# Two transformer layers on one core: packing the attention output for three of its four output projections

## The chip, the core and the metric

The kernel runs on one core of a Trainium2 chip. The core has a matrix engine (TensorE, "PE" in the profile; its weight loads are shown apart as "PEld"), three engines that work on vectors (VectorE or DVE, ScalarE or ACT, GpSimd or POOL) and a queue engine, SyncE or SP, which here issues almost all transfers. Each engine runs its own instructions in the order of the program and waits on semaphores for the others. TensorE writes its results to PSUM, which has eight banks of 128 partitions by 512 floats. The metric is the device time of one execution in microseconds, the median of the runs shown.

## The reference

The input x has 2048 rows of 448 floats. Twice, with the same weights, it goes through an attention layer and a gated feed-forward layer:

```
x = x + A(layernorm(x));  x = x + B(layernorm(x));  x = x + A(layernorm(x));  x = x + B(layernorm(x))

A(x): q = x @ wq            16 heads of 28
      k = x @ wk, v = x @ wv  one head of 28, shared by all query heads
      p = softmax(q k^T / sqrt(28));  o = p v
      return concat(o) @ wo   (448 -> 448)
B(x): (silu(x @ w_gate) * (x @ w_up)) @ w_down   (448 -> 1792 -> 448)
```

The change concerns the last line of A, `concat(o) @ wo`, and the norm behind it.

## The kernel before, in words

**Attention.** The 2048 rows are cut into four chunks of 512 rows (c = 0..3), and the 16 heads into four groups of four heads. A chunk and a head group make one of the 16 entries of `GR`; the loop in `scores` calls them i = 4c + g, and this text calls an entry a group. For each group the loop makes 16 steps (kt = 0..15), one for each block of 128 keys, so a layer has 256 steps, numbered n = 16 i + kt. A step makes the scores of four heads (`step`, L639: twelve matmuls, each in a strip of 32 rows of the array), and ScalarE takes their exponential: three heads at once from the PSUM tile `three` (L646, L652), the fourth from a bank of its own (L651 in even steps; in odd steps VectorE copies it to `raw`, L648, and ScalarE reads that, L649). Two steps make a pair d. `pv` (L680) multiplies the exponentials of the pair before by the values and VectorE adds the result to the group's accumulator `o` (L687 for the first pair, L690 after it). A column of ones beside the values makes the 29th row of each head the softmax's sum.

**The end of a group.** `post` (L701) sends the four rows of sums to `rs` over SP's queue. Three pairs later, at kt = 5 of the following group, `rest` runs: VectorE makes five short checks and a reciprocal of `rs` (L707 to L709), SP sends it out and brings it back spread over the partitions (`rd<-rs` L711, `o<-rd` L712), and GpSimd multiplies (L719) and splits the result into a rounded high part and a low part (`split`, L139 and L140). In before they go to `onh` and `onl`, in the row block of the group: head j of the group stands in partitions 32j to 32j+27, and the four partitions behind it are spare.

**Output projection.** When the last group of a chunk is through, the chunk is put on `todo`. `between(d)`, which is called at the end of each odd step, takes it off at kt = 10 and issues `outproj` for the four tiles of 128 rows: 4 head groups x 3 products (high x high, high x low, low x high) = 12 matmuls a tile over 128 partitions, whose spare rows meet zeros in `woh` and `wol`; 48 matmuls in all (L622), followed by four additions to the residual `xres` on VectorE (L626). They stand in the program between two pairs. This happens for the chunks 0, 1, 2, in groups 4, 8 and 12. The fourth chunk's projection comes after the loop and is not part of the change, apart from the name of its tile. The weights come in at kt = 8 of groups 2 and 3 (`load_wo`): GpSimd clears the buffer `wr`, SP loads it in four transfers, GpSimd splits it.

**The next norm.** The table `later` holds, by step number, the parts of the feed-forward's norm of a chunk: four `stat` steps on VectorE (L240, L241), `scale` on GpSimd (`rstd`, L246 and L247), four times `apply` (L255) and `turn` (a transpose, L260) on VectorE, then `send` and `load` over SP's queue and, for chunks 0 and 1, eight conversions on VectorE. In before they begin at the first step of the group behind the projection, 16 (4c + 5).

**What sets the order.** Each engine keeps the order in which the code issues. Transfers of SP's queue are issued in that order too; an SP instruction that waits holds back those behind it. The queries of a group come over the same queue: `stack(i + 2)` loads `qraw` at kt = 12 (L443), `parts(i + 1)` splits it on GpSimd at kt = 0, and `rows(i + 1)` adds four rows at kt = 3 (L454). In groups 11, 12 and 13 `weights` loads feed-forward weights at kt = 8 into the same `wr` and splits them in twelve GpSimd instructions.

Of the kernel before, what the change touches and what calls it, by code (L numbers as in the profile page):

```python
# [9 lines left out]
F32R = mybir.dt.float32r  # L10
AF = mybir.ActivationFunctionType
ALU = mybir.AluOpType
# [40 lines left out]
def forward(  # L53
# [315 lines left out]
    class Attention:  # L369
# [230 lines left out]
        def scores(self, ff):  # L600
            next(switch)
            with tc.tile_pool(name=f"at{self.layer}", bufs=1, reuse_waits="tile") as wp:
# [3 lines left out]
                todo, due = [], {}  # L606
                single = lambda d: banks[6 + d % 2]

                def load_wo(z):
                    r = wpool.tile([P, 4, 2, P], F32, name="wr").rearrange("p (z k) b n -> p z (k b n)", z=2)  # L610
                    nc.gpsimd.memset(r, 0.0)
                    for j in range(4):
                        nc.sync.dma_start(r[32 * j : 32 * j + DH, :, 0:D], wos[j][:, 2 * z : 2 * z + 2, :])
                    zs = slice(2 * z, 2 * z + 2)
                    split(woh[:, zs, :], wol[:, zs, :], r[:, :, 0:D])

                def outproj(c, t, po, gs=range(NG)):
                    oh, ol = on[c]
                    ts_ = slice(P * t, P * t + P)
                    for g in gs:  # L620
                        for z, (a, b) in enumerate(((oh, woh), (oh, wol), (ol, woh))):
                            nc.tensor.matmul(  # L622
                                po[:, 0:D], a[:, g, ts_], b[:, g, :], start=(g + z == 0), stop=(g == NG - 1 and z == 2)
                            )
# [69 lines left out]
                def post(i):  # L694

                    c, g = GR[i]
                    out2 = accs.pop(i)
                    oraw, rb = out2[:, 0, :], out2[:, 1, :]
                    rs = wp.tile([P, 16], F32, name="rs", bufs=2)
                    for j in range(4):  # L700
                        nc.sync.dma_start(rs[32 * j : 32 * j + 32, :], oraw[32 * j + DH : 32 * j + DH + 1, :])  # L701

                    def rest():
                        if fine is not None:
                            under = wp.tile([P, 16], F32, name="under", bufs=2)
# [5 lines left out]
                        nc.sync.dma_start(rd.rearrange("j (p n) -> (j p) n", n=16), rs)  # L711
                        nc.sync.dma_start(rb, rd[:, None, :].to_broadcast([4, 32, 512]))  # L712
                        if g == 0:
                            on[c] = (
                                wp.tile([P, NG, 512], F32R, name="onh"),
                                wp.tile([P, NG, 512], F32R, name="onl"),
                            )
                        oh, ol = on[c]
                        nc.gpsimd.tensor_tensor(rb, oraw, rb, ALU.mult)  # L719
# [21 lines left out]
                for n in range(last):  # L741
# [580 lines left out]
```

## Time and profile before

| | |
|---|---|
| median of three runs | 1959.17 us (1959.09 to 1959.79) |
| the profiled execution's own time | 1959.78 us |
| its span, first to last instruction | 1958.0 us |
| share of the span in which TensorE is busy | 99% |
| ScalarE | 68% |
| VectorE | 52% |
| GpSimd | 40% |

The shares are averages over stages of different kinds. In the first layer the 256 attention steps lie between 61 and 565 us of the span, in the second between 1031 and 1535 us; the rest is projections of queries and the feed-forward layers. "Busy" for TensorE counts overlapping matmuls whose ends are modelled, so 99% does not say that it never waits: it is read together with what the other engines wait for.

### The profile page before, as it was taken

The page shows a single profiled execution, that of the slowest core. Times are in us where ns is not written, and L with a number is a line of the kernel's source. Part 1 is how long each engine was busy: PE and PEld are TensorE (multiplying, and loading weights), DVE is VectorE, ACT ScalarE, POOL GpSimd, SP SyncE. Part 2 cuts the span into 40 slices and gives each one's busy share as a digit, 9 for nine tenths or more (in the row PEclk, how much of TensorE's full clock was granted, in tenths as well). Part 3 has the DMA queues.
Part 4 walks back from the last instruction along what each step waited for, and adds up shares of the span by engine and source line. Part 5 has one row for each costly group of instructions (what it writes and reads, how often), then busy time and mean ns, then how long its engine had stood idle before and what let it go on. Part 6 is the DMA issues. An engine that isn't in the chain of part 4 may idle for free. (4 is left out here: it accounts for less than half of the span.)

```text
span 1958.0 us, 45644 instructions
## 1 busy us (share of the span) xinstructions
PE 1946.5 (99%) x18307; PEld 1312.0 (67%) x18307; DVE 1016.5 (52%) x1711; ACT 1338.3 (68%) x2353; POOL 774.2 (40%) x997
## 2 busy tenths in 40 slices
PE   9999999999999999999999999999999999999998
PEld 8544545445458899999984444454454688999997
DVE  7444543544425567665654335445454346666653
ACT  4899797998963344444349998979979533444432
POOL 5212111132314868766441221111232167688640
PEclk9999999999999999999999999999999999999999
DMA  5110020121210110111131011102121101110002
GB/s 167 54 30 26 23 49 22 31 59 28 73 33 2 53 32 21 28 32 27 52 114 33 27 31 31 45 12 62 30 53 48 33 7 48 33 32 22 27 17 77
DMA packets 100017, 79.69 MB, mean 41 GB/s; under 512 B 26040, under 2 KB 83000, under 8 KB 99800
## 3 DMA queue, kind: packets, MB, share of 16 engines
q1 hardware_dynamic: 99224, 75.81, 14.2%
q8 instruction: 144, 2.36, 0.5%
q10 hardware_dynamic: 576, 0.92, 0.1%
q14 instruction: 73, 0.60, 0.1%
HBM read 57.15 MB, written 18.74 MB: 39 GB/s over the span
## 5 line engine op out<-in xcount | busy, mean ns | idle before, releaser
L680 PE MATMUL bank<-pt,vsb 128*32 128x512 f32 x4096 | 493.3, 598 | 0.3
L639 PE MATMUL bank<-qstack,keys 32*128 32x512 f32 x1536 | 484.5, 425 | 0.0
L639 PE MATMUL three<-qstack,keys 32*128 32x512 f32 x4608 | 460.2, 425 | 1.5 <-DVE vt L573 1.2
L639 PEld LDWEIGHTS three<-qstack,keys 32*128 32x128 f32 x4608 | 254.0, 182 | 295.4 <-ACT pt L652 178.6
L646 ACT ACTIVATE pt<-three 128x1536 f32<-128x1536 f32 x256 | 372.2, 1454 | 1.2 <-PE bank L680 0.8
L652 ACT ACTIVATE pt<-three 128x1536 f32<-128x1536 f32 x256 | 372.0, 1453 | 0.0
L358 PE MATMUL bank<-xh,wgh 64*128 64x512 f32 x1344 | 355.0, 392 | 0.3 <-DVE sg L1119 0.3
L358 PE MATMUL bank<-wdh,h 64*128 64x448 f32 x1776 | 324.3, 364 | 0.1
L648 DVE COPY raw<-bank 128x512 f32<-128x512 f32 x256 | 177.1, 692 | 226.8 <-PE bank L639 223.9
L358 PE MATMUL bank<-xh,wgl 64*128 64x512 f32 x1020 | 286.2, 390 | 0.0
L690 DVE TENSOR_TENSOR o<-bank,o 128x512 f32<-128x512 f32 x224 | 154.9, 692 | 240.5 <-PE bank L680 235.6
L719 POOL TENSOR_TENSOR o<-o 128x512 f32<-128x512 f32 x32 | 41.3, 1290 | 593.5 <-DMA o<-rd 462.1
L680 PEld LDWEIGHTS bank<-pt,vsb 128*32 128x32 f32 x4096 | 107.1, 109 | 249.9 <-issue 153.3
L365 ACT COPY seen<-bank 128x1 f32<-128x1 f32 x788 | 99.3, 163 | 244.4 <-PE bank L358 183.7
L358 PE MATMUL bank<-xl,wgh 64*128 64x512 f32 x912 | 247.9, 390 | 0.0
L639 PEld LDWEIGHTS bank<-qstack,keys 32*128 32x128 f32 x1536 | 243.3, 183 | 1.3 <-DVE o L690 0.6
L358 PEld LDWEIGHTS bank<-wdh,h 64*128 64x128 f32 x1776 | 225.9, 184 | 11.0 <-issue 2.0
L358 PE MATMUL bank<-wdl,h 64*128 64x448 f32 x888 | 204.7, 366 | 0.0
L358 PEld LDWEIGHTS bank<-xh,wgh 64*128 64x128 f32 x1344 | 191.5, 184 | 13.5 <-issue 0.9
L905 POOL TENSOR_TENSOR xres<-stage,xres 128x448 f32<-128x448 f32 x120 | 152.1, 1280 | 112.0 <-ACT stage L898 111.8
L651 ACT ACTIVATE pt<-bank 128x512 f32<-128x512 f32 x256 | 151.4, 592 | 60.8 <-PE bank L639 60.6
L870 DVE TENSOR_TENSOR xn<-bank,xn 128x512 f32<-128x512 f32 x192 | 126.5, 687 | 124.9 <-PE bank L358 94.2
(205 smaller groups left out, 3064.4 us busy)
## 6 DMA issues: line engine op xcount, KB each, us to landing
o<-rd SPq DMA_DIRECT2D x32, 256.0 KB
qraw<-qd SPq DMA_DIRECT2D x128, 56.0 KB
qd<-stage SPq DMA_DIRECT2D x30, 224.0 KB
xt<-xn SPq DMA_DIRECT2D x28, 224.0 KB
wdr<-in_B_w_down_dram SPq DMA_DIRECT2D x28, 224.0 KB
wr<-in_B_w_gate_dram SPq DMA_DIRECT2D x32, 192.0 KB
wr<-in_B_w_up_dram SPq DMA_DIRECT2D x32, 192.0 KB
xn<-xt SPq DMA_DIRECT2D x6, 768.0 KB
```

The lines of the kernel that those rows point to most:

```text
L358: nc.tensor.matmul(po, a, b, start=start, stop=stop, skip_group_check=True)
L365: nc.scalar.copy(seen[:, i : i + 1], po[:, 0:1])
L639: nc.tensor.matmul(three[:, j, :] if j < 3 else one, k[js, kp, ks], q[js, part, :], start=(z == 0), stop=(z == 2), tile_position=(32 * j, 0),)
L646: nc.scalar.activation(pt, three, AF.Exp, scale=SCALE)
L648: nc.vector.tensor_copy(raw, one)
L651: nc.scalar.activation(pt1, one, AF.Exp, scale=SCALE)
L652: nc.scalar.activation(pt, three, AF.Exp, scale=SCALE)
L680: nc.tensor.matmul(po[32 * j : 32 * j + 32, :], vsb[:, n % NT, :], pts[n][j], start=(n == 2 * d), stop=(n > 2 * d), skip_group_check=True,)
L690: nc.vector.tensor_tensor(acc, in_turn(po), acc, ALU.add)
L719: nc.gpsimd.tensor_tensor(rb, oraw, rb, ALU.mult)
L870: plus = lambda out, po, r: tt(by_tile(out), in_turn(po), by_tile(r), ALU.add)
L905: nc.gpsimd.tensor_tensor(r, h[e, t], r, ALU.add)
```

## The change

1. Heads 14 and 15 of a chunk (56 rows) no longer have a row block of their own: once the last group of the chunk is split, `spread` copies them in 14 transfers of four partitions each into the spare partitions: twelve fill the row blocks 0, 1 and 2, so that each holds 128 rows that matter, and two go to the lower half of block 3, which then holds 64 rows that matter. A 15th transfer copies that lower half to partitions 64 to 127. High and low parts share one tile `on` now, so that a transfer takes both.
2. The projection of the chunks 0, 1, 2 (`dense`) takes a tile of 128 rows with nine matmuls over 128 partitions and three over 64. The 64-row matmuls of two tiles are issued in turn, one in the lower and one in the upper half of the array. In the first pair of tiles they come last, in the second first, so that the twelve stand in one block.
3. The projection moves from kt = 10 of the group behind the chunk to kt = 2 of the next but one (groups 5, 9, 13).
4. The norm's `stat` steps begin four steps later than before, and all behind them eleven steps later.
5. The weights are loaded twice: packed for the three chunks (8 and 12 transfers in groups 2 and 3, no clearing, splits at the steps 13 and 15), and in the old form for the fourth chunk (group 14, cleared, four transfers at kt = 2 and four at kt = 12, splits five to eight steps on).

SP's queue behind the last group of chunk 0. The names are: `rd<-rs` and `o<-rd` the reciprocal's way, `qraw` the queries of the next group but one, `rs` the sums of the next group, `on<-on` the new copies. Before:

```order
L711 DMA rd<-rs 128x16 [waits DMAHW4_49,DMAHW5_49,DMAHW3_49,DMAHW6_49,DMAHW0_49,DVE_49]
L712 DMA o_2022<-rd 128x1x512 [waits DMAHW1_49,DMAHW0_49]
L443 DMA qraw<-qd_1_410 28x512 [waits DMAHW2_49]
L443 DMA qraw<-qd_1_410 28x512 x3
L701 DMA rs<-o_2399 32x1x16 [waits DVE_49]
```

After:

```order
L767 DMA rd<-rs 128x16 [waits DMAHW2_49,DMAHW4_49,DMAHW1_49,DMAHW7_49,DMAHW0_49,DVE_49]
L768 DMA o_2026<-rd 128x1x512 [waits DMAHW5_49,DMAHW4_49]
L124 DMA on<-on 4x1024 [waits DMAHW6_49,Pool_49]
L124 DMA on<-on 4x1024 x4
L124 DMA on<-on 4x1024 [waits DMAHW3_49]
...
L124 DMA on<-on 64x1024 [waits DMAHW4_49,DMAHW5_49,DMAHW3_49,DMAHW6_49,DMAHW2_49,DMAHW7_49,DMAHW1_49,DMAHW0_49]
L443 DMA qraw<-qd_1_410 28x512 x4
L757 DMA rs<-o_2412 32x1x16 [waits DVE_49]
```

The copies stand ahead of the next queries and the next sums; the first waits for GpSimd's split, and a DMAHW wait is for a transfer some eight places earlier, except for the last copy, which waits for all of them.

GpSimd from the split of group 12's output on, `wgh` and `wdl` being the feed-forward weights of group 13. Before:

```order
L246 TENSOR_SCALAR rstd<-mv 128x4 [waits DVE_49]
L247 TENSOR_TENSOR rstd<-rstd,halfn 128x4 [waits Pool_49]
L719 TENSOR_TENSOR o_5566<-o_5566 128x512 [waits DMAHW0_49]
L139 TENSOR_SCALAR onh<-o_5566 128x512 [waits Pool_49]
L140 TENSOR_TENSOR onl<-o_5566,onh 128x512 [waits Pool_49]
L139 TENSOR_SCALAR wgh<-wr 128x256 [waits DMAHW4_49,DMAHW1_49]
...
L140 TENSOR_TENSOR wdl<-wdr,wdh 128x224 [waits Pool_49]
```

After:

```order
L772 TENSOR_TENSOR o_5606<-o_5606 128x512 [waits DMAHW1_49,DVE_49]
L139 TENSOR_SCALAR on<-o_5606 128x512 [waits PE_49,Pool_49]
L140 TENSOR_TENSOR on<-o_5606,on 128x512 [waits Pool_49]
L139 TENSOR_SCALAR wgh<-wr 128x256 [waits DMAHW5_49,DMAHW2_49]
...
L140 TENSOR_TENSOR wdl<-wdr,wdh 128x224 [waits Pool_49]
L246 TENSOR_SCALAR rstd<-mv 128x4 [waits DVE_49]
L247 TENSOR_TENSOR rstd<-rstd,halfn 128x4 [waits Pool_49]
```

The norm's `rstd` for chunk 2 moves from ahead of the multiplication behind the twelve weight splits.

The core of the diff:

```diff
+                def spread(o):
+                    for q in range(14):
+                        p0 = 64 + 4 * q + 4 * (q > 6)
+                        dma(o[32 * (q % 4) + DH : 32 * (q % 4) + 32, q // 4], o[p0 : p0 + 4, 3])
+                    dma(o[64:128, 3], o[0:64, 3])
+
+                def dense(c, ts, pos, half_first):
+                    o = on[c]
+                    cols = [slice(P * t, P * t + P) for t in ts]
+                    terms = ((0, woh), (0, wol), (1, woh))
+
+                    def half():
+                        side_by_side(
+                            *(
+                                [
+                                    (po[:, 0:D], (o[rs, 3, v, cs], b[rs, 3, :]), half_first and z == 0, z == 2 and not half_first)
+                                    for z, (v, b) in enumerate(terms)
+                                ]
+                                for cs, po, rs in zip(cols, pos, HALVES)
+                            )
+                        )
+
+                    def full_tiles(cs, po):
+                        for g in range(3):
+                            for z, (v, b) in enumerate(terms):
+                                nc.tensor.matmul(
+                                    po[:, 0:D], o[:, g, v, cs], b[:, g, :],
+                                    start=(g + z == 0 and not half_first), stop=(g + z == 4 and half_first),
+                                    skip_group_check=True,
+                                )
...
+                    if half_first:
+                        half()
+                    for t, cs, po in zip(ts, cols, pos):
+                        full_tiles(cs, po)
+                        if half_first:
+                            add(t, po)
+                    if not half_first:
+                        half()
+                        for t, po in zip(ts, pos):
+                            add(t, po)
...
-                    if not todo or kt != 10:
+                    if not todo or kt != 2:
                         return
                     c = todo.pop()
-                    for f in [outproj(c, t, free[:, t, :]) for t in range(2)]:
-                        f()
-                    outproj(c, 2, one)()
-                    outproj(c, 3, single(d))()
+                    dense(c, (0, 1), (free[:, 0, :], free[:, 1, :]), False)
+                    dense(c, (2, 3), (one, single(d)), True)
...
                         nc.gpsimd.tensor_tensor(rb, oraw, rb, ALU.mult)
-                        split(oh[:, g, :], ol[:, g, :], rb)
+                        split(o[:, g, 0, :], o[:, g, 1, :], rb)
                         if g == NG - 1 and c < NC - 1:
+                            spread(o)
                             todo.append(c)
...
-                    n = NT * (4 * c + 5)
+                    n = NT * (4 * c + 5) + 4
                     for kt, f in enumerate(fs):
-                        later[n + kt] = f
+                        later[n + kt + (7 if kt > 3 else 0)] = f
+                    n += 7
                     later[n + 22] = got["load"]
...
                     if i in (2, 3) and kt == 8:
-                        load_wo(i - 2)
+                        later[n + 5], later[n + 7] = load_wo(i - 2, True)
+                    if i == 14 and kt in (2, 12):
+                        later[n + 7], later[n + 8] = load_wo(kt // 8, False)
```

More of the change, by code (lines that the diff above doesn't have):

```diff
@@ L607, in scores, with load_wo, cast @@
                 single = lambda d: banks[6 + d % 2]
-                def load_wo(z):
+                def load_wo(z, dense):
                     r = wpool.tile([P, 4, 2, P], F32, name="wr").rearrange("p (z k) b n -> p z (k b n)", z=2)
-                    nc.gpsimd.memset(r, 0.0)
+                    if not dense:
+                        nc.gpsimd.memset(r, 0.0)
+                    spare = wo[14 * DH : 16 * DH, :].rearrange("(q r) n -> r q n", r=4)
                     for j in range(4):
-                        nc.sync.dma_start(r[32 * j : 32 * j + DH, :, 0:D], wos[j][:, 2 * z : 2 * z + 2, :])
-                    zs = slice(2 * z, 2 * z + 2)
-                    split(woh[:, zs, :], wol[:, zs, :], r[:, :, 0:D])
+                        for up in (0, 64) if dense and z and j < 2 else (0,):
+                            own = slice(2 * z + bool(up), 2 * z + (1 if dense and z and j > 1 else 2))
+                            to = slice(bool(up), own.stop - 2 * z)
+                            p0 = up + 32 * j
+                            nc.sync.dma_start(r[p0 : p0 + DH, to, 0:D], wos[j][:, own, :])
+                            if dense:
+                                qs = slice(4 * own.start + j, 4 * own.stop - 3 + j, 4)
+                                nc.sync.dma_start(r[p0 + DH : p0 + 32, to, 0:D], spare[:, qs, :])
+                    def cast(a):
+                        split(woh[:, 2 * z + a, :], wol[:, 2 * z + a, :], r[:, a, 0:D])
+                    return [lambda: cast(0), lambda: cast(1)]
@@ new lines, in spread, with add @@
+                def spread(o):
[25 more added lines that the diff above has]
+                                )
+                    def add(t, po):
+                        x = xres[:, 4 * c + t, :]
+                        nc.vector.tensor_tensor(x, po[:, 0:D], x, ALU.add)
+                    if half_first:
[8 more added lines that the diff above has]
+                            add(t, po)
@@ L617, in outproj @@
                 def outproj(c, t, po, gs=range(NG)):
-                    oh, ol = on[c]
+                    oh, ol = (on[c][:, :, v, :] for v in range(2))
                     ts_ = slice(P * t, P * t + P)
@@ L713, in rest @@
                         if g == 0:
[L714 to L718, printed above, removed]
+                            on[c] = wp.tile([P, NG, 2, 512], F32R, name="on")
+                        o = on[c]
                         nc.gpsimd.tensor_tensor(rb, oraw, rb, ALU.mult)
-                        split(oh[:, g, :], ol[:, g, :], rb)
+                        split(o[:, g, 0, :], o[:, g, 1, :], rb)
                         if g == NG - 1 and c < NC - 1:
+                            spread(o)
                             todo.append(c)
```

## The prediction

> **What bounds it now.** I read the page first, then the busy time of the two attention stretches, then who waited for whom inside them, and last the six places at which the projections stand, in order of time.
>
> ```profile
> span 1958.0 us, 45644 instructions
> 61.00:565.00 504.00, 503.08 (x5259) 226.10 (x5254) 230.43 (x414) 473.55 (x513) 113.44 (x135) 1.00 0.14 36
> ```
>
> The second row is a stretch with the busy time of TensorE, its weight loads, VectorE, ScalarE and GpSimd, and behind them the granted clock (1.00). In the first layer's attention ScalarE works 473.6 of 504 us. Where the other 30 go, the waits tell; these are the rows for 60 to 600 and for 1050 to 1700 us (total, times, longest):
>
> ```profile
> ACT pt L651 <- PE bank L639: 29.6, 4, 9.9
> ACT pt L651 <- PE bank L639: 30.7, 3, 10.9
> ```
>
> Nearly all of ScalarE's idle time in attention is three waits per layer of about ten us, for the scores that stand behind a projection. Outside them it runs without a gap, so there is no second resource that would eat what a shorter projection saves. The first of them on ScalarE and on TensorE:
>
> ```profile
> 201.54 0.62 ACT L649 ACTIVATE pt<-raw 128x512 f32<-128x512 f32 x1
> 212.05 0.60 ACT L651 ACTIVATE pt<-bank 128x512 f32<-128x512 f32 x1 [9.89 <-PE bank L639]
> 201.18 0.36 PE L622 MATMUL three<-wol,onh 128*128 128x448 f32 x1
> 210.68 0.37 PE L622 MATMUL bank<-woh,onl 128*128 128x448 f32 x1
> ```
>
> From the second to the 48th matmul there are 46 intervals: (210.68 - 201.18) / 46 = 0.207 us each, and 48 of them are the 9.9 us of the wait. So what leaves this block leaves the end of the kernel, microsecond for microsecond.
>
> **The block itself.** 48 matmuls become 36 over 128 partitions and six pairs of halves. What a pair costs, and what going over from full rows to halves and back costs, stands ready in this trace behind the attention loop, where six pairs of 64-row matmuls of the same width (L358) lie between two runs of projection matmuls (L622):
>
> ```profile
> 578.32 0.36 PE L622 MATMUL bank<-wol,onh 128*128 128x448 f32 x1
> ...
> 585.20 0.37 PE L622 MATMUL bank<-woh,onl 128*128 128x448 f32 x1
> 585.50 0.47 PE L358 MATMUL bank<-wdh,h 64*128 64x448 f32 x2
> 585.81 0.36 PE L358 MATMUL bank<-wdl,h 64*128 64x448 f32 x2
> ...
> 586.63 0.37 PE L358 MATMUL bank<-wdh,h 64*128 64x448 f32 x2
> 586.92 0.47 PE L622 MATMUL bank<-woh,onh 128*128 128x448 f32 x1
> 587.23 0.36 PE L622 MATMUL bank<-wol,onh 128*128 128x448 f32 x1
> ```
>
> Full ones: (585.20 - 578.32) / 34 = 0.202. Pairs, the second to the sixth: (586.63 - 585.81) / 4 = 0.205, so a pair costs what one full matmul costs and the halves do run side by side. The whole from 585.20 to 587.23 is 2.03 us over eight intervals; at 0.2024 they would take 1.62. The two changes of shape cost the other 0.41. Now a block in the attention loop: at the slow pace 12 x 0.207 leave, 6 x 0.207 and 0.41 come: -0.83; at the fast pace 12 x 0.2024 against 6 x 0.205 + 0.41: -0.79. I take -0.81, and six blocks give **-4.9 us**. The bounds are -7.4 if the changes of shape cost nothing (6 x 6 x 0.205) and -2.4 if each costs twice as much. I take the middle because the row has the same six pairs between the same two neighbours.
>
> **The wait that goes away.** In the second layer's third block, TensorE meets a part that GpSimd has not split yet:
>
> ```profile
> 1427.34 1.29 POOL L719 TENSOR_TENSOR o<-o 128x512 f32<-128x512 f32 x1 [19.08 <-DMA o<-rd]
> 1430.75 0.47 PE L622 MATMUL three<-woh,onl 128*128 128x448 f32 x1 [0.68 <-POOL onl L140]
> 1439.53 0.60 ACT L651 ACTIVATE pt<-bank 128x512 f32<-128x512 f32 x1 [10.90 <-PE bank L639]
> 468.91 0.60 ACT L651 ACTIVATE pt<-bank 128x512 f32<-128x512 f32 x1 [9.70 <-PE bank L639]
> ```
>
> The block took ScalarE 10.90 us where the same block of the first layer, at the same pace, took 9.70. Moved by eight steps into the next group, it comes long after the split: **-1.2 us**. The five others did not wait, so nothing is to be had there.
>
> **The copies on SP's queue.** They hang between GpSimd's split and the projection. Chunk 0 of the first layer, where 179.68 opens group 4:
>
> ```profile
> 179.68 0.59 ACT L651 ACTIVATE pt<-bank 128x512 f32<-128x512 f32 x1
> 191.58 0.35 SPq L711 DMA_DIRECT2D rd<-rs  x1
> 193.01 0.57 SPq L712 DMA_DIRECT2D o<-rd  x1
> 198.31 1.30 POOL L719 TENSOR_TENSOR o<-o 128x512 f32<-128x512 f32 x1 [16.90 <-DMA o<-rd]
> 200.39 1.28 POOL L140 TENSOR_TENSOR onl<-o,onh 128x512 fp32r<-128x512 f32 x1
> 200.86 0.47 PE L622 MATMUL three<-woh,onh 128*128 128x448 f32 x1
> 576.89 1.18 SPq L124 DMA_DIRECT2D xd<-xh  x2
> ```
>
> The split ends 22.0 us into the group. The block begins 21.2 us into it at kt = 10, hence four pairs or 14.8 us earlier at kt = 2, in a group that starts 29.5 us later: at 35.9. No row shows a copy of four partitions. The nearest is `xd<-xh`, from SBUF to SBUF by the same line, 0.59 us on the queue each; `rd<-rs` is the cheapest, 0.35. A small transfer lands about 1.4 us after its issue (193.01 - 191.58, the second one waits for the first). At 0.59 the 14 copies are issued by 30.3, landed by 31.7; the 15th, 256 KB as `o<-rd`, lands after 5.3 us as that does (198.31 - 193.01), at 37.0. The full matmuls need the first twelve at 35.9, the halves need the 15th 18 matmuls later, at 39.6. Both are in time by 3 to 5 us, so I put the copies at **0**. By 0.35 the margin grows to 6; above, it is used up at about 0.59 + 2.6 / 14 = 0.78 us a copy (first rival). [...]
>
> What the copies push back on SP: the next queries and the next sums, by up to 10 us. The queries are split a group later for scores 29.5 us after that; the sums are read at kt = 5 of the next group, behind the moved block. Both stay covered; chunk 2 also carries seven weight loads there, some 4 us, and still does.
>
> **GpSimd.** The two clears and two pairs of splits move within groups 2 and 3 or return in groups 14 and 15; four half splits and two clears are new there.
>
> ```profile
> L140 POOL TENSOR_TENSOR wol<-wr,woh x4: 2110/2114/2123, 147.9 to 1147.2; 128x896 fp32r<-128x896 f32 x4
> 1524.39 1.29 POOL L719 TENSOR_TENSOR o<-o 128x512 f32<-128x512 f32 x1 [24.99 <-DMA o<-rd]
> ```
>
> The larger half of the split is 2.1 us, and GpSimd idles 25 us in that place: 0. Where GpSimd does get in the way is `rstd` of chunk 2, which now stands behind the weights of group 13:
>
> ```profile
> 1446.92 0.59 ACT L651 ACTIVATE pt<-bank 128x512 f32<-128x512 f32 x1
> 1446.53 0.62 DVE L240 BATCH_NORM_STATS2 stats<-xres 128x6 f32<-128x448 f32 x1
> 1447.74 0.69 DVE L648 COPY raw<-bank 128x512 f32<-128x512 f32 x1 [0.37 <-PE bank L639]
> 1449.63 0.69 DVE L690 TENSOR_TENSOR o<-bank,o 128x512 f32<-128x512 f32 x1 [0.45 <-PE bank L680]
> 1452.97 0.20 POOL L246 TENSOR_SCALAR rstd<-mv 128x4 f32<-128x4 f32 x1 [7.17 <-DVE mv L241]
> 1453.25 1.01 POOL L247 TENSOR_TENSOR rstd<-rstd,halfn 128x4 f32<-128x4 f32 x1
> 1475.73 0.68 POOL L140 TENSOR_TENSOR wdl<-wdr,wdh 128x224 fp32r<-128x224 f32 x1
> 1476.47 0.59 ACT L651 ACTIVATE pt<-bank 128x512 f32<-128x512 f32 x1
> ```
>
> 1446.92 opens group 13, 1476.47 group 14. The weights' splits end at 1476.41, as group 14 opens. In the changed kernel the block lies ahead of both, in the same group, so they shift together; `rstd` adds 1.3 us (1452.97 to 1454.26) and is there 1.25 us into group 14. The first `apply` stands on VectorE where 1446.53 stands, 0.4 us before a group opens. VectorE waits 1.6 us; then 0.5 of `apply`, and the copy to `raw`, due 0.8 into the group, comes about 1.0 late, the accumulation, due at 2.7, about 0.8 late. What lateness of that size costs, one place shows:
>
> ```profile
> 230.55 0.59 ACT L651 ACTIVATE pt<-bank 128x512 f32<-128x512 f32 x1
> 232.30 0.70 DVE L648 COPY raw<-bank 128x512 f32<-128x512 f32 x1
> 232.73 1.45 ACT L646 ACTIVATE pt<-three 128x1536 f32<-128x1536 f32 x1 [0.25 <-PE bank L680]
> 234.60 0.59 ACT L651 ACTIVATE pt<-bank 128x512 f32<-128x512 f32 x1
> ```
>
> The copy comes 1.75 us after the pair's start instead of 0.8, and the pair takes 4.05 us instead of 3.69: 0.36. Bounds: 0 and the full 1.6. I take 0.5 a layer, **+1.0 us**. For chunks 0 and 1 no weights stand there, and `rstd` is ready about 5 us ahead. The other norm steps are the same instructions a few steps later, with like collisions: 0 (a saving or loss of 0.4 a block is possible). The load for chunk 2's norm is issued a group before its use and still lands ahead of it.
>
> **Sum.** -4.9 - 1.2 + 1.0 = -5.1 us. The profiled execution took 1959.78 us, 1.8 beyond its span and 0.6 above the median of the runs; against it the sum gives 1954.7, against the median 1959.17 it gives **1954.1**.
>
> **Rivals.** (1) Slower: the copies do not overlap on SP's queue but follow each other at 1.43 us. Then the twelve for the full tiles are in at 22.0 + 17.2 = 39.2, 3.3 after the block's start, and the 15th lands at 22.0 + 20.0 + 5.3 = 47.3, 4.4 after the shifted halves: 7.7 us for each of six blocks, +46, about 2000 us. It decides from 0.78 us a copy on. For it: no row shows such copies, and the last waits for all. Against it: two `xd<-xh` are issued in 1.18 us without waiting for each other, and eight may be under way. Chance 0.10. (2) The halves do not run side by side in this block, since each writes another bank and reads another part of `on`: 12 instead of 6 intervals, no saving, and 0.41 a block to pay: +2.5 - 1.2 + 1.0, 1961.5 us. The rows of L358 speak against it. Chance 0.05. (3) VectorE's wait for `rstd` is passed on in full and in both layers, 3.2 instead of 1.0, and a changed norm collision takes a bit more: 1956.5, no change by measure. For it: TensorE has hardly any slack in a pair. Chance 0.17. The forecast keeps 0.68.
>
> **Numbers.** A measurement of this kernel tells about 0.2%, 3.9 us, from no change: faster means below 1955.25, slower above 1963.1. Of the forecast's 0.68, 0.03 lie above the first of these: faster 0.65; the same 0.23, from those, rival 3 and most of rival 2; slower 0.12, from rival 1 and from rival 2 where more comes on top. The range reaches from 1952.5 (no wait for `rstd`, shape changes at three quarters of their price) to 1957.3 (rival 3 with 0.4 more in two blocks), which leaves out rivals 1 and 2 and a few in a hundred more.
>
> **What the changed profile would show.** ScalarE's six waits drop from 9.7 to 10.9 us to about 8.9 to 9.1, all at kt = 2; the six pairs at L358 run at 0.205 with about 0.3 at either end; none of the block's matmuls waits for a transfer; VectorE's first `apply` of chunk 2 waits for GpSimd 1 to 2 us in both layers. A transfer as releaser ahead of a projection matmul, or VectorE waiting for `rs`, would make this wrong.

## The result and the profile after

| | median | runs |
|---|---|---|
| before, beside it | 1959.24 us | 18, from 1958.15 to 1960.26 |
| changed | 1955.26 us | 18, from 1954.45 to 1957.01 |
| ratio | 0.9981 | 95% interval 0.9974 to 0.9988 |

The change makes the kernel 4.0 us faster, 0.19%. The prediction called a time below 1955.25 us measurably faster, and 1955.26 lies on that line, though the interval lies wholly below 1. The forecast was 1954.1 us, so 1.2 us of the expected gain did not come. The profiled execution took 1955.75 us, 4.03 less than the one of before (1959.78). One run of e6 below took 7475.66 us for a reason that no record shows, and no median here depends on it.

The head of the page, and then ScalarE's waits for the scores between 60 and 600 us and between 1050 and 1700 us (total, times, longest), of the changed kernel:

```profile
span 1953.9 us, 45906 instructions
```

```profile
ACT pt L709 <- PE bank L697: 27.5, 5, 8.9
ACT pt L709 <- PE bank L697: 27.0, 4, 8.9
```

L709 and L697 are the old L651 and L639. The longest wait is 8.9 us instead of 9.9 and 10.9. In the second layer ScalarE also has new waits for other engines, which stand in rows of their own and are shown below.

One block in order of time, chunk 0 of the first layer. The lines are TensorE's: L654 are the full matmuls, L358 the halves, two in each pair, L697 the scores behind them.

```profile
215.62 0.47 PE L654 MATMUL three<-woh,on 128*128 128x448 f32 x1
...
219.23 0.37 PE L654 MATMUL three<-woh,on 128*128 128x448 f32 x1
219.53 0.47 PE L358 MATMUL three<-woh,on 64*128 64x448 f32 x2
219.84 0.36 PE L358 MATMUL three<-wol,on 64*128 64x448 f32 x2
...
220.65 0.37 PE L358 MATMUL bank<-woh,on 64*128 64x448 f32 x2
220.94 0.47 PE L654 MATMUL bank<-woh,on 128*128 128x448 f32 x1
221.25 0.36 PE L654 MATMUL bank<-wol,on 128*128 128x448 f32 x1
...
224.78 0.50 PE L697 MATMUL three<-qstack,keys 32*128 32x512 f32 x3
```

Six pairs take the place of twelve matmuls, each pair at (220.65 - 219.84) / 4 = 0.203 us. A change of shape shows as two intervals of 0.30, one before and one behind the first matmul of the new shape (219.23, 219.53, 219.84), so it costs 0.2. No row has a transfer as releaser. The block takes TensorE 9.16 us from 215.62 to 224.78.

To see where the time went I took, for both kernels, the start of each pair of steps (ScalarE's L651 and L709 in even steps). An undisturbed pair takes 3.69 us. What is above that:

| us beyond 3.69 a pair | before | changed | difference |
|---|---|---|---|
| three blocks, first layer | 9.99, 9.81, 9.80 | 9.04, 9.04, 8.98 | -2.54 |
| three blocks, second layer | 9.99, 9.98, 11.00 | 8.99, 8.97, 8.97 | -4.04 |
| first two pairs of group 14, both layers | none | 0.55 + 0.63, 1.56 + 0.63 | +3.37 |
| one pair of group 5 in each layer (norm against accumulation) | 0.36, 0.38 | none | -0.74 |

That is -4.0, which is what the profiled executions differ by. The blocks gave 6.6 us and the norm 0.7; 3.4 came back in one place, the opening of group 14. There the second layer reads (ScalarE, VectorE and GpSimd in order of time; L707 reads `raw`, L709 the bank, L710 and L704 the tile of three heads):

```profile
1470.26 0.59 ACT L709 ACTIVATE pt<-bank 128x512 f32<-128x512 f32 x1
1471.96 1.01 POOL L247 TENSOR_TENSOR rstd<-rstd,halfn 128x4 f32<-128x4 f32 x1
1473.01 0.81 DVE L255 TENSOR_SCALAR sg<-xres,mv,rstd 128x448 f32<-128x448 f32 x1 [3.06 <-POOL rstd L247]
1474.50 0.64 ACT L707 ACTIVATE pt<-raw 128x512 f32<-128x512 f32 x1 [0.97 <-DVE raw L706]
1475.51 0.60 ACT L709 ACTIVATE pt<-bank 128x512 f32<-128x512 f32 x1 [0.38 <-PE bank L697]
1477.96 1.45 ACT L704 ACTIVATE pt<-three 128x1536 f32<-128x1536 f32 x1 [0.50 <-PE bank L736]
```

VectorE stands 3.06 us before its first application of chunk 2's norm, because GpSimd delivers `rstd` at 1472.97, 2.71 us into the group. The copy to `raw` is queued behind it on VectorE, ScalarE waits for that copy, and through ScalarE the next scores and the next accumulation come late.

### The profile page after: what moved, and what is told of

Its sections match the earlier page's. It is cut to its first block, busy times and chain, and to the rows that moved or that the text cites. A ratio compares the mean times of both kernels' runs of the same rounds, so it can differ in the third digit from the quotient of the medians.

```text
span 1953.9 us, 45906 instructions
## 1 busy us (share of the span) xinstructions
PE 1940.9 (99%) x18307; PEld 1303.6 (67%) x18307; DVE 1020.0 (52%) x1711; ACT 1340.4 (69%) x2353; POOL 790.2 (40%) x1021
## 5 line engine op out<-in xcount | busy, mean ns | idle before, releaser
L697 PE MATMUL bank<-qstack,keys 32*128 32x512 f32 x1536 | 484.0, 425 | 2.3 <-DVE raw L706 1.4
L697 PE MATMUL three<-qstack,keys 32*128 32x512 f32 x4608 | 461.2, 424 | 1.5 <-DVE vt L573 1.2
L697 PEld LDWEIGHTS three<-qstack,keys 32*128 32x128 f32 x4608 | 254.0, 182 | 294.4 <-ACT pt L710 173.5
L704 ACT ACTIVATE pt<-three 128x1536 f32<-128x1536 f32 x256 | 372.5, 1455 | 1.7 <-PE bank L736 1.3
L710 ACT ACTIVATE pt<-three 128x1536 f32<-128x1536 f32 x256 | 372.1, 1454 | 0.0
L358 PE MATMUL bank<-xh,wgh 64*128 64x512 f32 x1344 | 360.6, 392 | 0.3 <-DVE sg L1176 0.3
L358 PE MATMUL bank<-wdh,h 64*128 64x448 f32 x1776 | 326.5, 364 | 0.1
L358 PE MATMUL bank<-xh,wgl 64*128 64x512 f32 x1020 | 289.4, 390 | 0.0
L358 PE MATMUL bank<-xl,wgh 64*128 64x512 f32 x912 | 252.0, 390 | 0.0
L697 PEld LDWEIGHTS bank<-qstack,keys 32*128 32x128 f32 x1536 | 243.3, 183 | 4.5 <-DVE raw L706 2.0
L358 PEld LDWEIGHTS bank<-wdh,h 64*128 64x128 f32 x1776 | 233.5, 184 | 10.8 <-issue 2.0
L358 PE MATMUL bank<-wdl,h 64*128 64x448 f32 x888 | 209.7, 366 | 0.0
L358 PEld LDWEIGHTS bank<-xh,wgh 64*128 64x128 f32 x1344 | 197.2, 184 | 13.4 <-issue 1.1
L709 ACT ACTIVATE pt<-bank 128x512 f32<-128x512 f32 x256 | 151.6, 592 | 54.9 <-PE bank L697 54.8
```

Source lines behind the costliest of these rows:

```text
L358: nc.tensor.matmul(po, a, b, start=start, stop=stop, skip_group_check=True)
L697: nc.tensor.matmul(three[:, j, :] if j < 3 else one, k[js, kp, ks], q[js, part, :], start=(z == 0), stop=(z == 2), tile_position=(32 * j, 0),)
L704: nc.scalar.activation(pt, three, AF.Exp, scale=SCALE)
L709: nc.scalar.activation(pt1, one, AF.Exp, scale=SCALE)
L710: nc.scalar.activation(pt, three, AF.Exp, scale=SCALE)
```

## Experiments

The theory: the blocks give what was worked out, and the late `rstd` of chunk 2 eats about half of it. The rivals in turn: the gain comes from where the block and the norm stand and not from the packing; the late pairs of group 14 have another cause; the copies matter. Every time below is a median, and each job ran before's kernel beside it: 1959.04 us (e1 to e4), 1959.08 (e5 to e8), 1959.09 (e9 to e11).

### e1: chunk 2's rstd ahead of the weight splits

```diff
                     fs, got = norm_steps(c, lambda: pers.tile([P, 512], F32, name="sg"))
+                    if c == 2:
+                        last_stat, rstd = fs[3], fs[4]
+                        fs[3] = lambda last_stat=last_stat, rstd=rstd: (last_stat(), rstd())
+                        fs[4] = lambda: None
```

> The changed kernel, with the rstd of chunk 2 computed in the same step as that chunk's last statistics, so that GpSimd does it ahead of the weight splits of group 13; chunks 0 and 1 keep their seven steps. Theory (group 14's late opening pairs are VectorE's first application of the norm, waiting for rstd behind those splits): the extra at the first pairs of group 14, 1.18 us in layer 0 and 2.19 us in layer 1, goes, VectorE's first application waits for no GpSimd instruction, and the kernel takes 1955.3 - 3.4 = about 1951.9 us. Rival (those pairs are late for another reason, such as the room that the applications themselves take on VectorE): the extra stays, 1955.3 us.

1953.59 us (1952.83 to 1954.04), ratio 0.9972, interval 0.9961 to 0.9983. The first two pairs of group 14 take 3.69 us in both layers, and nothing of GpSimd is left there as releaser. VectorE at that place, in the second layer:

```profile
1467.87 0.69 DVE L746 TENSOR_TENSOR o<-bank,o 128x512 f32<-128x512 f32 x1 [1.19 <-PE bank L736]
1468.48 0.62 DVE L255 TENSOR_SCALAR sg<-xres,mv,rstd 128x448 f32<-128x448 f32 x1
1469.68 0.69 DVE L706 COPY raw<-bank 128x512 f32<-128x512 f32 x1 [0.58 <-PE bank L697]
```

The application follows the accumulation at once. The two attention layers together are 3.4 us shorter than in the changed kernel's profile (496.84 and 496.86 us from the first pair's start to the last's, against 498.31 and 498.77), and the spans differ by 2.8. The medians differ by only 1.7: the profiled execution of the changed kernel was a late one, 0.5 above its median, and that of e1 an early one, 0.8 below its own. The 1951.9 us that were expected took the 3.4 of that late execution off the changed kernel's median. So the cause is settled, and the size is taken up under e9.

### e2: the old projection in the new place

```diff
-                    dense(c, (0, 1), (free[:, 0, :], free[:, 1, :]), False)
-                    dense(c, (2, 3), (one, single(d)), True)
+                    for f in [outproj(c, t, free[:, t, :]) for t in range(2)]:
+                        f()
+                    outproj(c, 2, one)()
+                    outproj(c, 3, single(d))()
...
-                            spread(o)
...
-                        later[n + 5], later[n + 7] = load_wo(i - 2, True)
-                    if i == 14 and kt in (2, 12):
-                        later[n + 7], later[n + 8] = load_wo(kt // 8, False)
+                        later[n + 5], later[n + 7] = load_wo(i - 2, False)
```

> The changed kernel with the old projection put back: 48 full matmuls a block, the old weight loads, no copies; the block stays after key tile 2 and the norm keeps its seven steps. Theory (the gain is the matmuls taken out): the wait of ScalarE behind each of the six blocks is 9.7 to 9.9 us again instead of 8.9 to 9.0, the openings of group 14 stay late by 1.2 and 2.2 us, and the time is 1955.3 + 6 x 0.8 = about 1960 us. Rival (the gain comes from where the block and the norm stand): the time stays at 1955 us, with waits below 9.2 us.

1959.96 us (1958.71 to 1964.23), ratio 1.0008, interval 0.9999 to 1.0017. The pairs with a block take 9.80, 9.79 and 9.98 us beyond 3.69 in the first layer and 9.80, 9.80 and 9.99 in the second. ScalarE's wait at the second layer's third block:

```profile
1452.90 0.60 ACT L709 ACTIVATE pt<-bank 128x512 f32<-128x512 f32 x1 [9.89 <-PE bank L697]
```

In before it was 10.90. So the move alone takes away TensorE's wait for GpSimd in that block (1.0 us), and the packing alone gives (59.17 - 53.99) / 6 = 0.86 a block. Without the packing the changed kernel is no faster than before: what the move gains, the late `rstd` takes. That one cost 0.6 and 3.7 us here. The 3.7 has a second part of 2.15 us in the pair behind, where the changed kernel lost 0.63. The busy time by stretch shows why (span of the stretch, TensorE, its weight loads, VectorE, ScalarE, GpSimd, granted clock), first at that place in the changed kernel, then here:

```profile
1477.00:1479.00 2.00, 2.00 (x24) 0.59 (x20) 1.81 (x3) 1.50 (x2) 0.00 (x0) 1.00 0.08 11
```

```profile
1481.00:1483.00 2.00, 2.00 (x13) 0.68 (x13) 0.60 (x1) 1.22 (x1) 0.00 (x0) 0.50 0.03 2
```

TensorE's granted clock fell to 0.50 behind two waits of 1.17 and 0.46 us, for 3.41 us; in the changed kernel it stayed at 1.00 behind two of 1.20 and 0.46. The same happened at this place in e3 and, in the first layer, in e7: there, too, the second pair loses 2.1 to 2.2 us. So the lower clock adds 1.5 us to what a late `rstd` costs by itself.

### e3: halves last in both pairs of row tiles

```diff
-                    dense(c, (2, 3), (one, single(d)), True)
+                    dense(c, (2, 3), (one, single(d)), False)
```

> The changed kernel with the half tiles last in the second pair of row tiles too, so that TensorE goes full, half, full, half in a block: four changes of matmul shape with the one back to the scores, instead of two. Theory (each change costs about 0.2 us, 0.41 us for the two that were seen): each of six blocks is 0.41 us longer, +2.5 us, about 1957.7 us, and each half stretch shows 0.3 us at both of its ends. Rival (the order within the block costs nothing, or the first halves of the second pair wait for something): no change, 1955.3 us.

1961.31 us (1960.91 to 1963.10), ratio 1.0013, interval 1.0004 to 1.0022: +6.1, where +2.5 was expected. The pairs with a block take 9.93 to 10.02 us beyond 3.69, +0.96 each. My count of changes was wrong: with the one back to the scores there are four instead of three, so that one change, 0.2 us, was to be expected. TensorE indeed needs 9.31 us for the block, 0.15 more. The rest, in order of time at the end of the first block:

```profile
224.90 0.37 PE L358 MATMUL bank<-woh,on 64*128 64x448 f32 x2
225.20 0.50 PE L697 MATMUL three<-qstack,keys 32*128 32x512 f32 x3
225.31 1.16 DVE L662 TENSOR_TENSOR xres<-bank,xres 128x448 f32<-128x448 f32 x2 [3.44 <-PE bank L358]
225.98 0.50 PE L697 MATMUL bank<-qstack,keys 32*128 32x512 f32 x1 [0.28 <-DVE xres L662]
227.04 0.60 ACT L709 ACTIVATE pt<-bank 128x512 f32<-128x512 f32 x1 [9.85 <-DVE stats L240]
```

With the halves last, both additions of the second pair of row tiles come after TensorE's last matmul, and the score's bank is free only when VectorE is through: the scores to `bank` start at 225.98 instead of 225.21. (The last row names a step of the statistics that ended at the same time; what ScalarE lacked are those scores.) In the changed kernel the first of the two additions is made while TensorE works on the fourth tile. That the halves of the second pair run first is therefore worth 0.96 us a block, 0.15 of it in TensorE's own time and the rest VectorE's additions.

### e4: each copy twice

```diff
-                        dma(o[32 * (q % 4) + DH : 32 * (q % 4) + 32, q // 4], o[p0 : p0 + 4, 3])
+                        for _ in range(2):
+                            dma(o[32 * (q % 4) + DH : 32 * (q % 4) + 32, q // 4], o[p0 : p0 + 4, 3])
```

> The changed kernel with each of the 14 small copies of four partitions issued twice, so that SP issues 29 copies a chunk instead of 15. Theory (SP issues one copy every 0.58 us and the block's halves wait for the last): the last copy is issued 8.1 us later, the first halves, now reached some 4 us after the block opens, wait 4 to 6 us for it, six blocks, +24 to +33 us, 1980 to 1988 us. Rival (the copies end with more than 8 us to spare): the waits of ScalarE stay at 8.9 us and the time at 1955.3 us.

2129.01 us (2127.06 to 2130.30), ratio 1.0867, interval 1.0852 to 1.0882: 29 us a block instead of 4 to 6. SP's queue, first of the changed kernel, then of this one:

```profile
201.31 11.13 SPq L124 DMA_DIRECT2D on<-on  x15
212.48 2.38 SPq L443 DMA_DIRECT2D qraw<-qd  x4
```

```profile
201.99 42.21 SPq L124 DMA_DIRECT2D on<-on  x29
```

The experiment did not do what I meant: a repeat writes where the copy before it writes, so it waits until that has landed. 14 pairs in 42.2 us are 3.0 us each, a copy that must land before the next goes. This is what the first rival of the prediction would have looked like, with 29 copies in place of 15; of the changed kernel's copies each keeps the queue for 0.58 us, one goes out every 0.62, and they overlap. What the doubled load alone costs had to be asked again (e7).

### e5: without the seven steps

```diff
-                        later[n + kt + (7 if kt > 3 else 0)] = f
+                        later[n + kt] = f
```

> The changed kernel without the seven steps: rstd and the applications of the norm follow their statistics at once, four steps after the block's key tile; the loads behind them stay. Theory (GpSimd reaches rstd only behind its multiplication of o, which waits for the transfer of rd, so VectorE's first application and the score copies behind it wait): some 7 us for chunks 0 and 1 and some 15 us for chunk 2 in each layer, +40 to +60 us, 1995 to 2015 us, with VectorE waiting for rstd. Rival (there is room, and the seven steps are not needed): 1955 us.

2023.84 us (2023.04 to 2024.90), ratio 1.0331, interval 1.0316 to 1.0347: +68.6, more than the 40 to 60 that were expected. New waits of 9.1, 9.6, 15.8 us in the first layer and 7.9, 8.5, 16.5 in the second, 67.4 in all. Chunk 2 of the first layer:

```profile
511.33 1.26 POOL L772 TENSOR_TENSOR o<-o 128x512 f32<-128x512 f32 x1 [10.84 <-DMA o<-rd]
521.91 1.01 POOL L247 TENSOR_TENSOR rstd<-rstd,halfn 128x4 f32<-128x4 f32 x1
522.95 0.51 DVE L255 TENSOR_SCALAR sg<-xres,mv,rstd 128x448 f32<-128x448 f32 x1 [13.92 <-POOL rstd L247]
527.74 1.45 ACT L704 ACTIVATE pt<-three 128x1536 f32<-128x1536 f32 x1 [14.97 <-PE bank L736]
```

GpSimd waits for its transfer, multiplies, splits weights and only then makes `rstd`; VectorE and all behind it stand still. The seven steps are a needed part of the move, and chunk 2 is where they are just too few.

### e6 and e11: all halves at the start of the block

e6 has the early `rstd` of e1 and calls `dense` once for all four tiles: both pairs of halves, then the full matmuls of the four tiles, each tile followed by its addition. e11 differs from e6 in one place:

```diff
-                        x = xres[:, 4 * c + t, :]
-                        nc.vector.tensor_tensor(x, po[:, 0:D], x, ALU.add)
+                        for u in ((), (0, 1), (2,), (3,))[t]:
+                            x = xres[:, 4 * c + u, :]
+                            nc.vector.tensor_tensor(x, pos[u][:, 0:D], x, ALU.add)
```

> The kernel with the early rstd of chunk 2, and both pairs of half tiles at the start of the block: TensorE goes half, full, scores, one change of matmul shape less than in the changed kernel. Theory (a change costs about 0.2 us, as the starts of the matmuls show): 6 x 0.2 = 1.2 us less than with the early rstd alone (1953.6), 1952.4 us, and no transfer among what the block waits for. Rival (the halves, now needed some 3.9 us sooner, wait for the last copies): the block opens late by up to 1 us, 1955 to 1960 us.

> The kernel with the halves at the start of the block, with VectorE's additions of the first two row tiles made after both of their full matmuls, so that TensorE does not wait between them. Theory (the 0.94 us between the first two row tiles was the addition, which reads the tile that TensorE writes next): the block's wait falls from 10.2 to about 9.3 us, 1960.4 - 6 x 0.94 = 1954.8 us. Rival (the halves at the start are slow for another reason): 1960 us.

e6: 1960.45 us, ratio 1.0007, interval 0.9997 to 1.0016, with 10.2 to 10.3 us beyond 3.69 in the pairs with a block. Neither side of the expectation was right: no copy is waited for, but TensorE stops between the first two tiles, here in the first block:

```profile
219.18 0.36 PE L652 MATMUL three<-woh,on 128*128 128x448 f32 x1
219.65 0.62 DVE L657 TENSOR_TENSOR xres<-three,xres 128x448 f32<-128x448 f32 x1 [3.05 <-PE three L652]
220.32 0.47 PE L652 MATMUL three<-woh,on 128*128 128x448 f32 x1 [0.79 <-DVE xres L657]
```

The first two tiles lie in one PSUM tile, `three`. A matmul into its second bank waits for VectorE's addition, which reads the first. From 219.18 to 220.32 is 1.14 instead of 0.20: 0.94 us in each block. e11 puts the addition behind both tiles: 1954.01 us, ratio 0.9975, interval 0.9966 to 0.9984, with 9.16 to 9.17 in those pairs. The cause is shown. One change of shape less still does not make it better than e1's 8.97 to 9.04: at the start of the block TensorE's halves into the last bank wait 0.3 us until VectorE has copied the accumulation out of it.

### e7: two passes of copies

```diff
-                    for q in range(14):
+                    for q in [*range(14), *range(14)]:
```

> The changed kernel with the 14 small copies made in two passes, so that no repeat waits for the copy that it repeats: SP issues 29 copies a chunk, the last 8.1 us later than in the changed kernel. Theory (a copy is issued every 0.58 us and lands some 2 us later, and the block has 3 to 7 us to spare): the third full tile of the first row tile waits about 2 us and the halves about 1 us, +2 to +3 us a block, +12 to +18 us, 1967 to 1973 us. Rival (the copies are slow one by one, as those that were repeated in place): 28 x 2.4 us, the block is over 40 us late, above 2150 us.

1987.22 us (1985.41 to 1990.17), ratio 1.0143, interval 1.0128 to 1.0159: +32, where +12 to +18 was expected. 29 copies are out after 20.07 us, 8.9 later than 15. The waits are where they were expected:

```profile
217.54 0.44 PE L654 MATMUL three<-woh,on 128*128 128x448 f32 x1 [0.65 <-DMA on<-on]
220.33 0.44 PE L654 MATMUL three<-woh,on 128*128 128x448 f32 x1 [1.95 <-DMA on<-on]
```

The matmuls of the third head group were reached at 217.3 without the waits and released at 220.3 by copies issued 8.9 us later, so in the changed kernel the copies have about 6 us to spare there; the prediction had 4 for the full matmuls. But the pair with this block is 4.7 us longer, more than the two waits. The busy time by stretch tells the rest (span of the stretch, PE, PEld, DVE, ACT, POOL, granted clock):

```profile
215.00:220.00 5.00, 2.73 (x18) 1.10 (x10) 0.71 (x2) 2.30 (x3) 0.00 (x0) 1.00 0.13 26
220.00:222.00 2.00, 1.67 (x6) 1.55 (x7) 0.00 (x0) 0.00 (x0) 0.00 (x0) 0.71 0.06 12
222.00:224.40 2.40, 2.40 (x8) 1.85 (x6) 0.00 (x0) 0.00 (x0) 0.00 (x0) 0.53 0.64 157
224.40:229.00 4.60, 4.60 (x28) 3.95 (x28) 1.78 (x3) 0.00 (x0) 1.91 (x2) 1.00 0.14 30
```

After the waits the granted clock is 0.50 for 3.41 us, and a matmul takes 0.37 us instead of 0.20. Eleven intervals there cost 1.5 us. The gaps cost 0.8 and 2.1: 4.5 of the 4.7.

But the lower clock is not what makes these blocks dear. Only three of the six show it, and their pairs take 13.28 to 13.73 us beyond 3.69. In the other three the full matmuls keep their 0.20, the halves then wait 1.08 to 1.26 us for the last copy, and the pairs take 13.45 to 13.75. So without the lower clock the last copy sets the end, at about the same time. That wait ends 3.0 us after the issue of the last copy. In the changed kernel that copy goes out at 211.90 and the halves begin at 219.53, so it has 4.6 us to spare; the prediction had 2.6, since it put the landing at 5.3. The six blocks make 27.4 of the 32 us; another 2.3 are lost in group 13 and 2.2 at the opening of group 14.

### e8, e9, e10: how much the late rstd costs

e8 and e10 are the changed kernel again, e9 is e1 again, on the same chip as e10.

> The changed kernel itself, beside the others on the same chip. If the difference of 1.7 us to the kernel with the early rstd is real, 1955.3 us here too; the profile shows how late rstd is this time, between 1 and 4 us in group 14 of each layer.

> The kernel with the early rstd of chunk 2 again, on one chip with the changed kernel. Theory (the changed kernel's times scatter by how late GpSimd comes to chunk 2's rstd, and without that wait they do not): 1953 to 1954 us with all runs within some 1.5 us, that is 2 to 4 us below the changed kernel's median on this chip. Rival (the chips differ): both kernels move together, less than 2 us apart, with like scatter.

> The changed kernel once more, for the comparison with the early rstd on one chip: 1955 to 1958 us with runs spread over 3 us or more by the theory of the late rstd; by the rival the spread and place of the kernel with the early rstd.

| | median | from, to | ratio | 95% interval |
|---|---|---|---|---|
| e8, changed | 1957.64 us | 1955.12, 1961.76 | 0.9994 | 0.9985 to 1.0003 |
| e10, changed | 1955.55 us | 1954.98, 1957.25 | 0.9982 | 0.9973 to 0.9991 |
| e9, early rstd | 1953.27 us | 1952.71, 1955.29 | 0.9972 | 0.9961 to 0.9982 |

The gain of the change itself is thus 4.0, 1.4 and 3.5 us in three jobs, and in that of e8 its interval reaches 1.

On one chip the early `rstd` is worth 2.3 us, and the openings of group 14 in e10's profile are late by 0.83 and 1.52, 2.35 together. That fits. The part of the theory about scatter does not hold: e9's runs spread as far as e10's. Why the runs of e8 reach up to 1961.8 us is not shown; its profile is of a run at 1955.2 and shows nothing unusual. But its two slowest runs, 1961.76 and 1959.66 us, are the two with the lowest mean granted clock, 0.997 and 0.998 against 0.999 to 1.000 in the others. So stretches at the lower clock, as e2 has one behind the late `rstd`, are a likely part of it.

The three profiles of the changed kernel give six openings of group 14. When `rstd` is ready, counted from the opening, and what the first two pairs lose:

| | after, 1st | after, 2nd | e8, 1st | e8, 2nd | e10, 1st | e10, 2nd |
|---|---|---|---|---|---|---|
| rstd ready, us into the group | 1.72 | 2.71 | 1.38 | 2.21 | 1.35 | 2.05 |
| lost, us | 1.18 | 2.19 | 0.86 | 1.68 | 0.83 | 1.52 |

The loss is the lateness less 0.53 us, each time, and it has two parts. The first pair loses the lateness less 1.15 us, in these six openings and in the eight of e2, e3, e4 and e7. The second pair loses 0.62 us however late `rstd` is: in e2's first layer it was ready 1.15 us into the group, the first pair lost nothing, and the second still lost 0.62. Where the granted clock fell the second pair lost 2.1 to 2.2.

## Why the prediction was right, and which term was wrong

**The blocks** were worked out at -0.81 each. They gave 0.86 (e2 against the changed kernel, same place, same norm). The halves run side by side, a pair takes 0.203 us, and either change of shape shows two intervals of 0.30, as read from the rows behind the attention loop. Rival 2 is out.

**The wait that goes away** was put at -1.2 and is 1.0, and e2 shows that it belongs to the move and not to the packing. The move takes 0.4 more off the other five blocks (59.17 against 60.57 for all six), which the prediction did not have.

**The copies** were put at 0, and are 0 (no transfer is a releaser; 4.6 to 6 us to spare by e7). Rival 1 is out, and e4 shows its form. The prediction took the copies to go out at about 0.59 us each and to overlap: they do, one every 0.62. Where one transfer must wait for another, the time adds up: a copy and its repeat take 3.0 us (e4), 2.4 without the second one's issue, and in the changed kernel the 15th copy, which waits for the others, goes out 2.41 us behind the 14th (209.49 and 211.90). Where copies may overlap, as the first 14 do here, it does not: they go out in 8.8 us.

**The rstd of chunk 2** was put at +1.0 and was the term that was mis-sized: 2.3 us by the medians of e9 and e10, 3.4 in the first profile. The place and the mechanism were right, down to VectorE's wait on GpSimd, though that is 2.06 and 3.06 us in the profile and 1 to 2 had been foretold. Two steps of the working failed. First, the lateness: 1.25 us was carried over from before. The chain hangs on VectorE's reciprocal, sent out as `rd<-rs`, and that is 17.86 us ahead of group 14 in both kernels. But what follows it did not take the same time. The second layer, before and then changed:

```profile
1458.61 0.36 SPq L711 DMA_DIRECT2D rd<-rs  x1
1460.05 0.55 SPq L712 DMA_DIRECT2D o<-rd  x1
1466.04 1.28 POOL L719 TENSOR_TENSOR o<-o 128x512 f32<-128x512 f32 x1 [11.78 <-DMA o<-rd]
```

```profile
1452.40 0.36 SPq L767 DMA_DIRECT2D rd<-rs  x1
1455.00 0.57 SPq L768 DMA_DIRECT2D o<-rd  x1
1461.29 1.30 POOL L772 TENSOR_TENSOR o<-o 128x512 f32<-128x512 f32 x1 [11.61 <-DMA o<-rd]
```

From the first issue to GpSimd's multiplication: 7.43 us before, 8.89 changed, and 1.25 + 1.46 = 2.71. In the first layer it is 7.87, and 1.25 + 0.44 = 1.69 (1.72 measured). The prediction had one sample of a transfer that varies. Second, the part that is passed on: it took 0.36 us, from a place where VectorE was late by 0.95, as the pattern. That was a single late copy. Here the copy, the next copy and the accumulation are all late, and 0.62 us are lost in the second pair on top of what the first passes on.

This is rival 3, as a mechanism: the wait is passed on nearly in full. Rival 3 had 3.2 us for it and a time of 1956.5. The measured 1955.26 lies between it and the forecast, because the wait cost 2.3 in the middle of the runs, and because the two small collisions of the norm behind the first block of each layer (0.36 and 0.38 us), which the prediction put at 0, are gone. That the total came out only 1.2 us above the forecast is in part luck: in the profiled execution the late `rstd` cost 2.4 us more than foreseen, and the blocks (0.5) and the norm (0.7), which gave more than foreseen, hid half of that. In e8 the same kernel took 1957.64 us, above the range of 1952.5 to 1957.3.

**The best kernel** of the study is e1, the changed kernel with four lines more: 1953.3 to 1953.6 us, 5.5 to 5.8 us below before.

## What to carry to other kernels

A change that takes work off the bounding engine should be checked for what it makes late: here 6.6 us were saved at the blocks and about a third to a half given back by one 1.3 us step on a mostly idle engine (GpSimd is busy for 40% of the span), because that step was queued behind 7 us of work that nobody needed soon. When a wait is carried from one profile to another, look how much its chain varies; one sample of a transfer is no bound (7.43 us in before, 8.89 in the changed kernel). And who reads a PSUM tile last is part of the order of the matmuls: the same instructions with the additions placed otherwise cost 0.8 to 0.9 us a block (e3, e6).

## What the runs showed of the hardware that was not expected

- TensorE's granted clock can fall to 0.50 after short waits: two of 0.65 and 1.95 us, with three matmuls between them, were followed by 3.41 us at 0.50 (e7), in which a matmul took 0.37 us instead of 0.20. Where the waits lie counts, and not their length alone: in the third block of e7 waits of 0.73 and 1.55 us were followed by it, in the second block 0.75 and 1.64 were not. Each stretch at 0.50 that begins and ends within the loops of e2, e4, e5 and e7 lasts 3.41 us or a whole multiple of it (3.41 in e2 and e7, 13.6 in e5, from 515.6 to 529.2), and within a trace they begin whole multiples of 3.41 us apart (e7: 220.86, 483.68, 524.64 and 1337.01, which lie 77, 12 and 238 times 3.413 apart). In that grid the waits of the third block fall almost wholly into one stretch, in which TensorE is busy for 1.38 of 3.41 us, and those of the second into two, the later with 1.77:

```profile
350.63:354.04 3.41, 1.77 (x9) 1.51 (x9) 0.00 (x0) 0.00 (x0) 0.00 (x0) 1.00 0.09 19
480.27:483.68 3.41, 1.38 (x6) 0.65 (x4) 0.59 (x1) 0.95 (x2) 0.00 (x0) 1.00 0.13 26
483.68:487.10 3.42, 3.18 (x9) 2.86 (x10) 0.00 (x0) 0.00 (x0) 0.00 (x0) 0.50 0.31 66
```

- `rd<-rs`, 8 KB, is through 1.4 to 1.5 us after its issue in the first layer's group 13 (the issue of `o<-rd`, which waits for it) and after 2.3 to 3.1 us in the second layer's, in ten profiles of kernels with the moved norm, and 1.82 and 1.70 us in the eleventh (e7); in before it took 1.44 there, and 2.69 one group earlier. It is not the four rows of queries sent shortly before it (in e2 those went out 15.7 us ahead, and it took 3.05). What it is stays open.
